# Row sums and pooled products of an attention kernel on 64x64 tiles of TensorE

## The chip, the cores and the metric

One core of a Trainium2 chip runs the whole program. The metric is the device time of one execution in microseconds; lower is better. The engines are TensorE (PE), VectorE (DVE), ScalarE (ACT), GpSimd (POOL) and SyncE (SP), which run side by side and wait for one another through semaphores. PEld is TensorE's loading of weights.

## The reference

The kernel computes two kinds of attention, adds them, and sends the sum through a feed-forward block. There are 8 batches with 8 heads, 576 positions and a head dimension of 64.

```python
def _attn_ref(q, k, v):                       # (8, 8, 576, 64)
    factor, scale = 4, 1 / sqrt(64)
    q_d, k_d, v_d = (x.reshape(B, H, 144, 4, D).mean(axis=3) for x in (q, k, v))
    out_up = np.repeat(sm_attn(q_d, k_d, v_d), 4, axis=2)   # attention of the pooled positions
    mask = np.abs(pos[:, None] - pos[None, :]) < factor     # a band of 7 positions
    scores = np.where(mask, scale * q @ k.T, -1e9)
    out_local = softmax(scores) @ v
    return out_up + out_local

def _moe_ref(x, w_in, w_out):                 # x: (4608, 512), d_ff 2048
    h = x @ w_in
    return (h * sigmoid(h)) @ w_out
```

## The kernel before

**Pairs.** Two heads are worked on together and called a pair; there are 32, p = 0 to 31, four to a batch. All matmuls of the attention are small and use parts of TensorE's array: a matmul on a 64x64 tile takes 64 rows of keys (or of the head dimension) and 64 output columns. In the code `half(j)` is the lower or upper 64 partitions.

For each pair TensorE transposes q and k (`pe_T`, into the PSUM banks `o0` and `pe_`), multiplies them (`pe_S`, into the banks A and B, which are the tile `AB`), and later multiplies the exponentials with v (`pe_main`). ScalarE copies the transposed k out (`ek`) and takes the exponentials `Pt` of the banded scores (unit `x`) and `Pd` of the pooled scores (unit `xd`). VectorE copies the transposed q out of `o0` (unit `eq`, line 362, `qT<-o`), pools k and q (`mk`, `mq`, lines 586 and 590) and multiplies `Pt` by the band's mask (unit `k`, line 628).

**The part that the change touches.** `pe_main` writes the banks C and D (the tile `CD`, 2 x 512 floats in each partition), which are the only ones for this from pair 4 on. For pair `pv` it multiplies the exponentials with v: 4 matmuls of the pooled remainder and 20 of the band, all on 64x64 tiles, where each half j of the keys has its own bank j; and then 4 "pooled products" that take all 128 keys at once (128x64 tiles, `vd[n][:, 2 * h, :]`). For pair `z` it forms the row sums of the exponentials with 14 matmuls against constant matrices of ones (`ohf`, `ohl`, `ohp`, `ohe`), also on 128x64 tiles, into columns 360 to 432 of bank C.

From the row sums, `after_Z` takes the reciprocal on VectorE (unit `r`, line 717 from pair 10 on, the constant `NDIR`), and ScalarE's queue writes it to a scratch tensor in DRAM (unit `z`, `scr<-zr`) and reads it back spread over the partitions (unit `b`, twice, `Rb<-scr`); the read is issued by ScalarE's queue after the write has landed, so what stands behind it on ScalarE waits too. For pairs below 10 another path without DRAM is used. `after_PV` multiplies the contents of C and D by `Rb` on VectorE into `xo` (unit `m`, line 745, 2 x 360 columns in one operation), and GpSimd adds the local and the pooled part into `xT` (unit `a`, line 769).

**The feed-forward block.** `g1(j, f)` multiplies 512 tokens of `xT` by 128 columns of `w_in` (4 matmuls into one of two banks `HP`), ScalarE takes the tanh (unit `t`, line 783), and VectorE forms the gated value (unit `s`, line 785, `gT<-th,HP`), which frees the bank. `g2` multiplies by `w_out`, four parts of 4 matmuls, into `o0` (or `pe_` for some of the last tokens); ScalarE copies the result out (unit `o`, line 800) and SyncE stores it.

**The order of the work.** From n = 10 on a step V(n) puts S(n), T(n+1), PV(n-2) and Z(n-1) into one unit on TensorE, in this order of matmuls: scores of pair n, transposes of pair n+1, products of pair n-2, row sums of pair n-1, pooled products of pair n-2. Between two steps stand about four `g1` units and the four parts of one `g2`; in steps up to V14 also a unit VP or RB. Every unit has a guessed cost, and a planner (`Plan.order`) plays through the program with these costs and gives each engine its list of units; the engines then run their lists in order. A list of names in `FIRST` fixes the beginning of an engine's list. Before the change `FIRST` is empty.

In the profile, all matmuls but the transposes stand at line 359, the transposes at line 572, and all DMA issues at line 464.

Of the kernel before, what the change touches and what calls it, by code (L numbers as in the profile page):

```python
# [6 lines left out]
ALU = mybir.AluOpType  # L7
# [12 lines left out]
NDIR = 10  # L20
# [141 lines left out]


FIRST = {
}

class Plan:
# [109 lines left out]
def bass_hourglass_attn__then__act_silu_kernel(  # L277
# [9 lines left out]
    with kctx:  # L287
        E = kctx.enter_context
        L = Plan()
        res = {}  # L290

        def R(name, psum=False):
            if name not in res:
                res[name] = Res(name, psum)
            return res[name]
# [5 lines left out]
        NQK, NVS, NVQ, NB, NX, NT, NP_, NV, NR = 4, 4, 2, 3, 2, 2, 4, 4, 3  # L301
# [13 lines left out]
        vd = sb("vd", [128, 4, 64], BF16, NV)  # L315
# [4 lines left out]
        Pt = sb("Pt", [128, 2, 288], BF16, NP_)  # L320
        Pd = sb("Pd", [128, 2, 216], BF16, NP_)
        zr = sb("zr", [128, 72], F32, 2)
        Rb = sb("Rb", [128, 720], F32, NR)
        xo = sb("xo", [128, 2, 360], F32, NX)
# [10 lines left out]
        ohl = sb("ohl", [128, 127], BF16)  # L335
        ohf = sb("ohf", [128, 64], BF16)
        ohp = sb("ohp", [128, 127], BF16)
        ohe = sb("ohe", [128, 64], BF16)
# [14 lines left out]
        def one(eng, name, cost, fn, r=(), w=(), dma=None, prio=None, dcost=0.0):  # L353
            u = L.unit(eng, name, cost, prio, dcost)
            L.op(u, fn, r, w, dma)
            return u

        def mm(u, out_, lhsT, rhs, r, w, start=True, stop=True):
            L.op(u, lambda t: t.matmul(out_, lhsT, rhs, start=start, stop=stop, skip_group_check=True), r, w)  # L359
# [6 lines left out]
        def half(j):  # L366
            return slice(64 * j, 64 * j + 64)
# [282 lines left out]
        def acc(p):  # L650
            return (HP, rH) if p < 4 and p % 2 else (CD_, rCD_)

        def pe_main(u, pv, z):
            fresh = set()

            def first(x, h):
                f = (x, h) not in fresh
                fresh.add((x, h))
                return f

            if pv is not None:
                m, n = pv % NP_, pv % NV
                CD, rCD = acc(pv)
                rd = [R(f"vd{n}0"), R(f"vd{n}1"), R(f"Pd{m}")]
                for h in range(2):
                    for j in range(2):
                        mm(u, CD[half(h), j, 288:360], vd[n][half(j), 2 * h + 1, :], Pd[m][half(j), h, 144:216],
                           rd, [rCD[j]], start=first(j, h), stop=False)
                for i in range(5):
                    for h in range(2):  # L670
                        for j in range(2):
                            a, e = 58 * i, min(58 * i + 58, 288)
                            mm(u, CD[half(h), j, a:e], vb[n][half(j), 5 * h + i, :],
                               Pt[m][half(j), h, a:e], [R(f"vb{n}"), R(f"P{m}")], [rCD[j]],
                               start=False, stop=True)
            if z is not None:
                m = z % NP_
                CD, rCD = acc(z)
                for s in range(4):
                    for h in range(2):  # L680
                        mm(u, CD[half(h), 0, 360:432], ohl[:, 63 - s:127 - s] if s else ohf[:, :],
                           Pt[m][:, h, 72 * s:72 * s + 72],
                           [R("ohl0"), R("ohl1"), R("ohf0"), R("ohf1"), R(f"P{m}")], [rCD[0]],
                           start=first(0, h), stop=False)
                for y in range(2):
                    for h in range(2):
                        mm(u, CD[half(h), 0, 360:432], ohp[:, 59 - 5 * y:123 - 5 * y], Pd[m][:, h, 72 * y:72 * y + 72],
                           [R("ohp"), R(f"Pd{m}")], [rCD[0]], start=False, stop=False)
                for h in range(2):
                    mm(u, CD[half(h), 0, 360:432], ohe[:, :], Pd[m][:, h, 144:216],  # L690
                       [R("ohe0"), R("ohe1"), R(f"Pd{m}")], [rCD[0]], start=False, stop=True)
            if pv is not None:
                m, n = pv % NP_, pv % NV
                CD, rCD = acc(pv)
                for y in range(2):
                    for h in range(2):
                        mm(u, CD[half(h), y, 288:360], vd[n][:, 2 * h, :], Pd[m][:, h, 72 * y:72 * y + 72],
                           [R(f"vd{n}0"), R(f"vd{n}1"), R(f"Pd{m}")], [rCD[y]], start=False, stop=True)

        def after_Z(p):  # L700
            i, u = p % 2, p % NR
            CD, rCD = acc(p)
            if p < NDIR:
                (h, m, l), rp = [rpart[p % 2][:, k, :] for k in range(3)], rpr[p % 2]
                zs, rest, rz = zr[i][:, :], rrest[p % 2][:, :], R(f"rrest{p % 2}")
                sg = [R("sgn0"), R("sgn1")]
                one("DVE", f"r{p}", 0.56, lambda e: e.reciprocal(zs, CD[:, 0, 360:432]), r=rCD[:1], w=[R(f"zr{i}")],
                    prio=-400000)
                one("ACT", f"rh{p}", 0.25, lambda e: e.activation(h, zs, AF.Copy), r=[R(f"zr{i}")], w=[rp[0]],
                    prio=-400000)  # L710
                one("DVE", f"rx{p}", 0.2, lambda e: e.scalar_tensor_tensor(  # L711
                    rest, h, sgn[:, 0:1], zs, ALU.mult, ALU.add), r=[R(f"zr{i}"), rp[0]] + sg, w=[rz], prio=-400000)
                one("DVE", f"rm{p}", 0.15, lambda e: e.tensor_copy(m, rest), r=[rz], w=[rp[1]], prio=-400000)
                one("DVE", f"rl{p}", 0.2, lambda e: e.scalar_tensor_tensor(  # L714
                    l, m, sgn[:, 1:2], rest, ALU.mult, ALU.add), r=[rz, rp[1]] + sg, w=[rp[2]], prio=-400000)
                return
            one("DVE", f"r{p}", 0.56, lambda e: e.reciprocal(zr[i][:, :], CD[:, 0, 360:432]),
                r=rCD[:1], w=[R(f"zr{i}")], prio=-400000)
            eng = "ACT"
            dma(eng, f"z{p}", scr[u][0:74, :], zr[i][0:74, :], [R(f"scr{u}")], f"scr{u}", 0.2, r=[R(f"zr{i}")], prio=-500000)  # L720
            for h in range(2):
                src = bass.AP(tensor=scr[u].tensor, offset=scr[u].offset + 64 * h * 72, ap=[[0, 64], [1, 720]])
                dma(eng, f"b{p}", Rb[u][half(h), :], src, [R(f"Rb{u}{h}")], f"Rb{u}{h}", 0.85,
                    r=[R(f"scr{u}")], prio=-500000)
# [17 lines left out]
        def after_PV(p):  # L742
            u, x = p % NR, p % NX
            CD, rCD = acc(p)
            one("DVE", f"m{p}", 0.92, prio=-450000 if L.boost else None, r=rCD + [R(f"Rb{u}0"), R(f"Rb{u}1")], w=[R(f"xo{x}")], fn=lambda e: e.tensor_tensor(  # L745
                xo[x][:, :, :], CD[:, :, 0:360], Rb[u][:, :].rearrange("p (x n) -> p x n", x=2), ALU.mult))
            b, kc = divmod(p, 4)
            t = b * S_
            segs = []
            wrap = (t // XR + 1) * XR - t  # L750
            if wrap >= S_:
                segs.append((0, S_))
            else:
                cuts = sorted({0, 288, wrap, S_})
                segs += list(zip(cuts, cuts[1:]))
            for a, e_ in segs:
                n = e_ - a
                d0 = (t + a) % XR
                dst = xT[:, kc, d0:d0 + n].bitcast(F32R)
                if n == S_:  # L760
                    dst = dst.rearrange("p (y g r) -> p y g r", y=2, r=4)
                    in0 = xo[x][:, :, 0:288].rearrange("p y (g r) -> p y g r", r=4)
                    in1 = xo[x][:, :, 288:360].unsqueeze(3).to_broadcast([128, 2, 72, 4])
                else:
                    y, c = divmod(a, 288)
                    dst = dst.rearrange("p (g r) -> p g r", r=4)
                    in0 = xo[x][:, y, c:c + n].rearrange("p (g r) -> p g r", r=4)
                    in1 = xo[x][:, y, 288 + c // 4:288 + (c + n) // 4].unsqueeze(2).to_broadcast([128, n // 4, 4])
                one("POOL", f"a{p}", 0.15 + n * 0.0019, lambda g, dst=dst, in0=in0, in1=in1: g.tensor_tensor(  # L769
                    dst, in0, in1, ALU.add), r=[R(f"xo{x}")], w=xblk(kc, t + a, t + e_), prio=-200000)  # L770
# [147 lines left out]
        n = 10  # L918
# [54 lines left out]
```

The softmax here doesn't subtract the row's maximum and nothing guards it: scores larger than these inputs give would overflow.

## Time and profile before

| what | value |
|---|---|
| median of 4 runs | 356.66 us (355.72 to 357.14) |
| the profiled execution's own time | 356.28 us |
| its span, from first to last instruction | 354.5 us |
| mean granted clock of TensorE | 0.97 |
| busy: PE, DVE, ACT, POOL | 329.7, 227.3, 181.0, 156.6 us |
| VectorE's reciprocal, line 717 | 22 times, 606 ns each |
| VectorE's product, line 745 | 30 times on CD, 901 ns each |
| step from V19 to V20 (152.75 to 161.41 us) | 8.66 us |

The profile is of one execution. Busy time counts from the start to the end of an instruction; matmuls overlap one another, so a busy TensorE is not one at its peak. The windows give the busy time of each engine in a stretch. A row of the timeline merges neighbouring instructions of one kind: start, time, engine, line, operation, output<-input, tile rows*columns, shape, count, and in brackets the idle time before it and who ended it. "Step" below is the time from one V's first matmul to the next one's.

### The profile page before, as it was taken

To read this page: it belongs to the slowest core of one execution; us is meant where nothing else is said; L and a number is where in the kernel's file an instruction comes from. 1 tells how busy PE (TensorE), PEld (TensorE's weight loads), DVE (VectorE), ACT (ScalarE), POOL (GpSimd) and SP (SyncE) were. 2 spreads that over 40 slices of the span, in tenths; PEclk is the share of its full clock that TensorE was granted. 3 is DMA by queue.
4 is the path that set the end of the run, shared out by engine and by line. 5 is a ranking of instruction groups with operands and counts; after the bars stand their busy time and mean duration, and the time that the engine had idled before them with its cause. 6 is when DMAs were issued, how large, how long until landed. Compare 5 with 4: busy or idle time off the path is not lost.

```text
span 354.5 us, 11025 instructions
## 1 busy us (share of the span) xinstructions
PE 329.7 (93%) x4742; PEld 214.6 (61%) x4742; DVE 227.3 (64%) x392; ACT 181.0 (51%) x326; POOL 156.6 (44%) x203
## 2 busy tenths in 40 slices
PE   1575699999999999999999999999999999999996
PEld 0464577766666666666666666666655666666642
DVE  7587889876677787877777667777754433333400
ACT  2766478766554555554555454555534343434321
POOL 7876974362556575575467654755111100000000
PEclk9995589999999999999999999999999999999999
DMA  8889999956788777777887778773122000100012
GB/s 238 238 241 270 314 296 223 228 131 199 208 220 218 227 220 223 219 213 214 228 231 206 217 219 224 214 199 96 66 97 75 31 30 30 60 31 30 31 59 89
DMA packets 73506, 60.28 MB, mean 170 GB/s; under 512 B 47986, under 2 KB 55794, under 8 KB 73458
## 3 DMA queue, kind: packets, MB, share of 16 engines
q1 hardware_dynamic: 63818, 44.27, 46.5%
q10 hardware_dynamic: 5416, 9.02, 8.5%
q0 software_dynamic: 4224, 6.29, 7.7%
q8 instruction: 37, 0.61, 0.7%
q14 instruction: 11, 0.09, 0.1%
HBM read 51.76 MB, written 9.91 MB: 174 GB/s over the span
## 4 chain that ended last, share of the span: by engine, by line
PE 85%; DVE 7%; ACT 2%; POOL 2%; DMA 1%; issue 1%; ACTq 0%; DVEq 0%
PE HP L359 38%; PE o L359 27%; PE pe_ L359 8%; PE CD L359 5%; PE AB L359 4%; POOL xo L382 2%; PE o L572 1%; DMA scr<-zr 1%; DVE rrest L711 1%; DVE gT L785 1%; DVE rp L714 1%; DVE xo L745 1%; DVE Pt L628 1%; ACT th L783 1%; PE pe_ L572 1%
## 5 line engine op out<-in xcount | busy, mean ns | idle before, releaser
L359 PE MATMUL HP<-xT,w_in_sb 128*128 128x512 f32 x576 | 159.9, 416 | 1.0 <-DVE gT L785 0.9
L785 DVE SCALAR_TENSOR_TENSOR gT<-th,HP 128x512 bf16<-128x512 f32 x144 | 96.4, 684 | 99.3 <-ACT th L783 99.3
L359 PEld LDWEIGHTS HP<-xT,w_in_sb 128*128 128x128 f32 x576 | 106.0, 189 | 28.4 <-DVE gT L785 1.4
L783 ACT ACTIVATE th<-HP 128x512 f32<-128x512 f32 x144 | 85.9, 599 | 72.8 <-PE HP L359 71.0
L359 PE MATMUL o<-w_out_bf,gT 128*128 128x512 bf16 x464 | 107.0, 380 | 0.0
L359 PEld LDWEIGHTS o<-w_out_bf,gT 128*128 128x128 bf16 x464 | 42.6, 98 | 54.3 <-issue 7.8
L769 POOL TENSOR_TENSOR xT<-xo 128x576 fp32r<-128x576 f32 (+3 forms) x48 | 44.7, 945 | 43.7 <-DVE xo L745 43.6
L800 ACT ACTIVATE osb<-o 128x512 f32<-128x512 f32 x29 | 17.4, 599 | 63.4 <-PE o L359 52.3
L559 POOL TENSOR_TENSOR vt<-vq 128x512 f32<-128x512 f32 x18 | 23.0, 1280 | 55.0 <-DMA vq<-in_v_dram 55.0
L544 POOL CAST qkb<-qk 128x1152 bf16<-128x1152 f32 x30 | 34.6, 1154 | 8.1 <-PE pe_ L572 4.0
L745 DVE TENSOR_TENSOR xo<-CD,Rb 128x720 f32<-128x720 f32 x30 | 27.0, 901 | 1.2 <-ACT Rb L735 0.9
L359 PE MATMUL pe_<-w_out_bf,gT 128*128 128x512 bf16 x112 | 26.4, 380 | 0.0
L554 POOL CAST vb<-vs 128x640 bf16<-128x640 f32 x30 | 21.6, 720 | 10.3 <-PE CD L359 5.2
L572 PE MATMUL o<-idn,qkb 64*64 64x64 bf16 x576 | 17.8, 205 | 8.4 <-DVE qkb L539 6.3
L586 DVE TENSOR_REDUCE kd<-kT 128x144 bf16<-128x576 bf16 x32 | 23.4, 733 | 1.1 <-ACT kT L582 1.1
L582 ACT ACTIVATE kT<-pe_ 128x576 bf16<-128x576 bf16 x32 | 21.0, 657 | 1.6
L628 DVE TENSOR_TENSOR Pt<-Pt,mask_bf 128x576 bf16<-128x576 bf16 x32 | 21.3, 667 | 0.5 <-ACT Pt L624 0.5
L624 ACT ACTIVATE Pt<-AB 128x576 bf16<-128x576 f32 x32 | 20.8, 650 | 1.2 <-PE AB L359 1.2
L572 PEld LDWEIGHTS o<-idn,qkb 64*64 64x64 bf16 x576 | 14.3, 119 | 9.2 <-DVE qkb L539 6.3
L572 PE MATMUL pe_<-idn,qkb 64*64 64x64 bf16 x576 | 16.7, 205 | 1.9 <-DVE qkb L541 1.0
L359 PEld LDWEIGHTS pe_<-w_out_bf,gT 128*128 128x128 bf16 x112 | 10.0, 98 | 13.6 <-issue 3.2
L590 DVE TENSOR_REDUCE qd<-qT 128x144 bf16<-128x576 bf16 x24 | 17.8, 742 | 0.0
(79 smaller groups left out, 316.2 us busy)
## 6 DMA issues: line engine op xcount, KB each, us to landing
vs<-in_v_dram SPq DMA_DIRECT2D x126, 80.0 KB, 4.4
qk<-in_q_dram SPq DMA_DIRECT2D x32, 288.0 KB, 3.9
out_dram<-osb SPq DMA_DIRECT2D x36, 256.0 KB, 3.2
qk<-in_k_dram SPq DMA_DIRECT2D x30, 288.0 KB, 4.8
Rb<-scr ACTq DMA_DIRECT2D x44, 180.0 KB, 4.1
vq<-in_v_dram SPq DMA_DIRECT2D x18, 256.0 KB, 4.7
w_in_sb<-in_moe_w_in_dram POOLq DMA_DIRECT2D x4, 1024.0 KB, 10.0
w_out_bf<-in_moe_w_out_dram POOLq DMA_DIRECT2D x4, 512.0 KB, 10.5
```

Of the source, the lines that this page charges most:

```text
L359: L.op(u, lambda t: t.matmul(out_, lhsT, rhs, start=start, stop=stop, skip_group_check=True), r, w)
L544: one("POOL", f"c{p}", 1.15, lambda g: g.tensor_copy(qkb[j][:, :, :], qk[i][:, :, :]), r=[R(f"qk{i}0"), R(f"qk{i}1")], w=[R(f"qkb{j}0"), R ...
L554: one("POOL", f"cw{p}", 0.72, lambda g: g.tensor_copy(vb[m][:, :, :], vs[i][:, :, :]), r=rr, w=[R(f"vb{m}")])
L559: one("POOL", f"va{p}", 1.3, lambda g: g.tensor_tensor(vt[:, :, :], vq[i][:, :, 0:128], vq[i][:, :, 128:256], ALU.add), r=rr, w=[R("vt")])
L572: L.op(u, lambda e, o=o, w=w, j=j: e.transpose(o, w, idn[half(j), :]), [R("id"), R(f"qkb{n}{x}")], [rE if x else rF])
L582: one("ACT", f"ek{p}", 0.68, lambda e: e.activation(kT[j][:, 3:579].rearrange("p (g r) -> p g r", r=9), pe_[:, 0:288].bitcast(BF16).rearra ...
L586: one("DVE", f"mk{p}", 0.74, lambda e: e.tensor_reduce(kd[j][:, 0:SD], kT[j][:, 3:579].rearrange("p (g r) -> p g r", r=4), AX.X, ALU.add), ...
L628: one("DVE", f"k{p}", 0.46, lambda e: e.tensor_tensor(Pt[m][:, :, :], Pt[m][:, :, :], mask_bf[:, :].unsqueeze(1).to_broadcast([128, 2, 288 ...
L745: one("DVE", f"m{p}", 0.92, prio=-450000 if L.boost else None, r=rCD + [R(f"Rb{u}0"), R(f"Rb{u}1")], w=[R(f"xo{x}")], fn=lambda e: e.tenso ...
L769: one("POOL", f"a{p}", 0.15 + n * 0.0019, lambda g, dst=dst, in0=in0, in1=in1: g.tensor_tensor(dst, in0, in1, ALU.add), r=[R(f"xo{x}")], w ...
L783: one("ACT", f"t{j}_{f}", 0.62, lambda e: e.activation(th[tb][:, :], hps[hb], AF.Tanh, scale=0.5), r=[rH[hb]], w=[R(f"th{tb}")], prio=-1)
L785: one("DVE", f"s{j}_{f}", 0.71, lambda e: e.scalar_tensor_tensor(gT[j % 2][:, f, :], th[tb][:, :], 1.0, hps[hb], ALU.add, ALU.mult), r=[rH ...
```

## The change

From pair 10 on, the row sums and the pooled products are formed on 64x64 tiles: each of the 18 matmuls becomes two, one for each half of the keys, and each half writes its own bank. Row sums now lie in columns 432 to 504 of both banks, pooled products in columns 288 to 432 of both (four matmuls of the pooled remainder move there as well). The pooled products now come before the row sums. VectorE adds the two halves: the unit `r` becomes copy, add, reciprocal; the unit `m` becomes copy, add and product of the pooled part, and the product of the rest. `FIRST` is filled with a list of names for each engine, up to the middle of step V11. The planner's cost of `r` goes from 0.56 to 0.9, that of `m` from 0.92 to 1.4.

```diff
 FIRST = {
+    "PE": """T0 T1 S0 T2 S1 Z0 ... V11 g1_1_6 g1_1_7 VP10 g2_0_1_0 g2_0_1_1""",
+    "ACT": ..., "DVE": ..., "POOL": ..., "SP": ...
 }
...
                 for h in range(2):
                     for j in range(2):
-                        mm(u, CD[half(h), j, 288:360], vd[n][half(j), 2 * h + 1, :], Pd[m][half(j), h, 144:216],
+                        c = 288 + 72 * j if pv >= NDIR else 288
+                        mm(u, CD[half(h), j, c:c + 72], vd[n][half(j), 2 * h + 1, :], Pd[m][half(j), h, 144:216],
                            rd, [rCD[j]], start=first(j, h), stop=False)
...
-            if z is not None:
+            if pv is not None and pv >= NDIR:
+                for y in range(2):
+                    for h in range(2):
+                        for j in range(2):
+                            mm(u, CD[half(h), j, 288 + 72 * y:360 + 72 * y], vd[n][half(j), 2 * h, :],
+                               Pd[m][half(j), h, 72 * y:72 * y + 72], rd, [rCD[j]], start=False, stop=True)
+            if z is not None and z >= NDIR:
+                ...
+                parts = [(ohl[:, 63 - s:127 - s] if s else ohf[:, :], Pt[m][:, :, 72 * s:72 * s + 72]) for s in range(4)]
+                parts += [(ohp[:, 59 - 5 * y:123 - 5 * y], Pd[m][:, :, 72 * y:72 * y + 72]) for y in range(2)]
+                parts.append((ohe[:, :], Pd[m][:, :, 144:216]))
+                for i, (o, x) in enumerate(parts):
+                    for h in range(2):
+                        for j in range(2):
+                            mm(u, CD[half(h), j, 432:504], o[half(j), :], x[half(j), h, :], ro, [rCD[j]],
+                               start=first(j, h), stop=i == 6)
+            elif z is not None:
...
-            if pv is not None:
+            if pv is not None and pv < NDIR:
...
-            one("DVE", f"r{p}", 0.56, lambda e: e.reciprocal(zr[i][:, :], CD[:, 0, 360:432]),
-                r=rCD[:1], w=[R(f"zr{i}")], prio=-400000)
+            q = L.unit("DVE", f"r{p}", 0.9, -400000)
+            L.op(q, lambda e: e.tensor_copy(zr[i][:, :], CD[:, 0, 432:504]), rCD[:1], [R(f"zr{i}")])
+            L.op(q, lambda e: e.tensor_tensor(zr[i][:, :], zr[i][:, :], CD[:, 1, 432:504], ALU.add),
+                 [R(f"zr{i}"), rCD[1]], [R(f"zr{i}")])
+            L.op(q, lambda e: e.reciprocal(zr[i][:, :], zr[i][:, :]), [R(f"zr{i}")], [R(f"zr{i}")])
...
+            q = L.unit("DVE", f"m{p}", 0.92 if p < NDIR else 1.4, -450000 if L.boost else None)
...
+                pool = [CD[:, j, 288:432].rearrange("p (y n) -> p y n", y=2) for j in range(2)]
+                xp = xo[x][:, :, 288:360]
+                L.op(q, lambda e: e.tensor_copy(xp, pool[0]), rCD[:1], wx)
+                L.op(q, lambda e: e.tensor_tensor(xp, xp, pool[1], ALU.add), [rCD[1]] + wx, wx)
+                L.op(q, lambda e: e.tensor_tensor(xp, xp, rb[:, :, 288:360], ALU.mult), rr + wx, wx)
+                L.op(q, lambda e: e.tensor_tensor(xo[x][:, :, 0:288], CD[:, :, 0:288], rb[:, :, 0:288], ALU.mult),
+                     rCD + rr, wx)
```

## The prediction

> **What bounds the kernel now.** I read the page first: is there an engine that never rests, and where?
>
> ```profile
> span 354.5 us, 11025 instructions
> ...
> PE   1575699999999999999999999999999999999996
> ...
> PEclk9995589999999999999999999999999999999999
> ...
> PE 85%; DVE 7%; ACT 2%; POOL 2%; DMA 1%; issue 1%; ACTq 0%; DVEq 0%
> ```
>
> From slice 7 (53 us) TensorE is busy in every slice, at a full granted clock, and is 85% of the chain that ended last. From there each microsecond taken from TensorE's own work is a microsecond of the span, unless another engine then comes late. I count on the span of 354.5 us; that execution took 356.28 us, 1.8 outside the span, which I leave unchanged. The median of the runs, 356.66, is 0.4 higher.
>
> The change acts in the stage of the steps V12 to V33, one every 8.65 us. The windows of two neighbouring steps show how much slack the others have:
>
> ```profile
> 152.75:161.41 8.66, 8.66 (x140) 5.60 (x140) 6.23 (x10) 4.04 (x9) 5.17 (x5) 1.00 0.80 226
> 161.41:170.10 8.69, 8.69 (x140) 5.61 (x139) 6.39 (x11) 4.94 (x10) 5.12 (x5) 1.00 0.82 216
> ```
>
> PE (second number) fills the step; VectorE (fourth) works 6.2 to 6.4 us, so some 2.3 us are free. Inside a step, the timeline of PE at the end of V19:
>
> ```profile
> 153.31 0.21 PE L359 MATMUL CD<-Pd,vd 64*64 64x72 bf16 x4
> 153.34 0.34 PE L359 MATMUL CD<-Pt,vb 64*64 64x58 bf16 x20
> 153.61 0.22 PE L359 MATMUL CD<-Pt,ohf 128*64 128x72 bf16 x2
> ...
> 153.86 0.23 PE L359 MATMUL CD<-Pd,vd 128*64 128x72 bf16 x4
> 154.03 0.50 PE L359 MATMUL HP<-xT,w_in_sb 128*128 128x512 f32 x1
> ```
>
> The single records show three things. The 24 matmuls on 64x64 tiles start in rounds of four, 32 ns apart, also the round with 72 columns (153.311 to 153.343). The last starts at 153.492, and then nothing starts until 153.613, where the 128x64 tiles begin. These start in nine pairs, the last at 153.894. A start-to-start gap of 119 to 122 ns stands at this turn in nearly every step. The turn into the 128x128 matmuls behind costs 128 ns from 128x64 and 123 to 141 ns from 64x64 (the two such places), so that one stays.
>
> **TensorE, part by part.** The change puts pool and row-sum matmuls on 64x64 tiles: 18 become 36, and the turn falls away.
> - The turn: the next round would have started at about 153.502 instead of 153.613: -0.111 us.
> - Streaming: nine pairs took 0.281 us from first to last start (the first step 52 ns, the rest 33); nine rounds of four at 32 ns take 0.256: -0.025. Bounds: never under the 31 ns a round that the transposes of the same step reach; above, if only two ran at a time as now, 18 steps of 33 ns, +0.30. I take 32 ns, since the round with 72 columns is the same shape with the same tile order.
> - Sum: -0.13 us a step. V12 to V33 lose the turn, 22 steps: -2.9 us. In V11 the pool part of pair 9 still has its turn, so nothing there. The lists in FIRST name units up to V11 in the order of the trace of before; nothing to gain or lose.
>
> The Trainium skill speaks against such splitting: "TensorEngine Tiling (Array Packing)", section Instruction Overhead, gives each matmul about 60 cycles whatever its columns, and warns against tiling a dimension that is already small. By an estimate from that page, 18 more matmuls charged one after the other at 2.4 GHz would add 0.45 us a step, some 10 us in all; the 32 ns rounds above say that four share that time.
>
> **VectorE.** Its step is back to back around the turn:
>
> ```profile
> 152.88 1.30 DVE L785 SCALAR_TENSOR_TENSOR gT<-th,HP 128x512 bf16<-128x512 f32 x2 [1.52 <-ACT th L783]
> 154.11 0.61 DVE L717 RECIPROCAL zr<-CD 128x72 f32<-128x72 f32 x1
> 154.63 0.70 DVE L362 COPY qT<-o 128x576 bf16<-128x576 bf16 x1
> ...
> 157.75 0.90 DVE L745 TENSOR_TENSOR xo<-CD,Rb 128x720 f32<-128x720 f32 x1
> 158.56 0.54 DVE L628 TENSOR_TENSOR Pt<-Pt,mask_bf 128x576 bf16<-128x576 bf16 x1
> ```
>
> The unit r (reciprocal) gets a copy and an add ahead of it. No row has these sizes. The product L745 (720 elements) takes 901 ns and L785 (512) 684, both reading PSUM: 217 ns for 208 elements, 1.04 ns each, and some 150 ns fixed, so 0.226 us for 72 elements. The copy L362 (576 elements in 694 ns) has 95 fixed: 0.17. So 0.17 to 0.23 for the copy, 0.23 for the add. Each result is read by the next one, which waits. How that looks, early in the kernel:
>
> ```profile
> 17.32 0.29 DVE L711 SCALAR_TENSOR_TENSOR rrest<-rp,sgn,zr 128x72 f32<-128x72 bf16 x1
> 17.65 0.73 DVE L713 CAST rp<-rrest 128x72 bf16<-128x72 f32 x1
> 18.41 0.29 DVE L714 SCALAR_TENSOR_TENSOR rp<-rp,sgn,rrest 128x72 bf16<-128x72 bf16 x1
> ```
>
> A dependent one starts 35 ns after the end of the last; independent ones start 80 ns before it (154.63 against 154.11 + 0.61). So r grows by 0.17..0.23 + 0.035 + 0.23 + 0.035 = 0.47 to 0.53 us; I take 0.50. Below, a reciprocal that reads SBUF instead of PSUM might be up to 0.1 shorter; above, with GpSimd busy the same small SBUF operations ran to 0.73 (L713, alone 0.18), so up to 0.8.
>
> The skill's "VectorE: DVE Perf Modes", section The DRAIN you can't avoid, says that a semaphore between chained operations costs nothing extra. The rows above show about 115 ns for each such wait; by the page r would grow by 0.27 only.
>
> The unit m becomes four dependent operations: 144-element copy 0.25 to 0.30, add 0.30, product 0.30, 576-element product 0.75, with three gaps of 0.035; 1.67 us to the next start instead of 0.82: +0.85, and up to 1 more in a step where its SBUF product meets GpSimd (L711, the same kind, ran from 0.28 to 3.25). Cover: the 2.3 us free behind the mask product in each step. r and m together take 1.35 of it. Behind m stand the mask product (read by the next V, 2 us later), GpSimd's sum into xT (wanted after the next V at the latest, with which it can change places), and the release of CD (next written 2.5 us later). I cost m at nothing; were its cover gone by 1 us more, the next step would start late by that.
>
> **Where r counts.** Behind r on VectorE stands the copy of qT out of bank o, which the second GEMM wants next. From the start of V: r starts at 1.35 us (the product ahead of it ends then, held by ScalarE's tanh, so an earlier end of V does not help it), the copy ends at 2.57, seen by PE 0.05 later; the GEMM's first matmul starts at 3.22 to 3.25. Slack 0.615. After the change the GEMM would start 0.13 earlier: slack 0.485 against a growth of 0.47 to 0.53. So a stall of 0 to 0.05, mean 0.02, in the 16 steps without VP (V12 to V14 have it between) and before V31: +0.3 us.
>
> Second, r releases the row-sum write to scr, on whose landing ScalarE's queue waits, with tanh behind it. The write was issued 2.0 us into V and landed at 4.6 to 5.2 mostly, at 6.8 to 6.9 in three steps. The chain of waits shows one:
>
> ```profile
> 198.04 4.93 DMA scr<-zr
> ...
> 204.79 0.49 ACT th L783
> ...
> 205.31 0.70 DVE gT L785
> ```
>
> A landing past about 6.3 delays the next step's tanh, gT, and r; there r started 0.4 to 0.5 late, which the slack of 0.615 swallowed. Now the write goes out at 2.5. In the three steps where that was so already (161.4, 204.7, 222.1) it landed at 5.6 to 5.9, in time. But if one lands at 7.4, 0.5 past those of now, r starts some 1.0 late (0.45, that 0.5, and the shorter step), and as its growth has used the slack, all of it reaches the GEMM. I allow one such step, a little under 1.0: +0.9.
>
> Sum: -2.9 + 0.3 + 0.9 = -1.7 us. On 356.28 this gives 354.6, on the median 355.0; I say 354.8.
>
> **The rivals.** *All of it is cover*: r grows under 0.485 and no landing is late: -2.9, 353.4 us. For it: the regular steps repeat to 10 ns and the sums meet almost exactly. *The landing decides* (the slower side): the scr write, now issued behind the q and k loads that SP starts at 2.0 and 2.4, lands past 6.3 in more steps. Each costs about 1.0; from four on the change is slower. Five: -2.9 + 0.3 + 5.0 = +2.4, 358.7 us. For it: the three landings at 6.8 to 6.9; against: the three writes issued late that landed in time. *r is too long*: at a growth of 0.8 the GEMM waits 0.315 in 16 steps, +5.0 - 2.9: 358.4 us; it turns slower at 0.67. Against: GpSimd is mostly idle 1.8 to 2.3 us into V. *The tiles don't overlap*: two at a time, (0.30 - 0.11) x 22 = +4.2, 360.5 us; the rounds of four speak against it.
>
> **How the numbers follow.** Forecast 0.35, all cover 0.28, landing 0.17, r too long 0.12, no overlap 0.05, else 0.03. A measurement of this kernel can tell about 0.3% (1.1 us) from no change. All of the cover case and most of the forecast are faster by more: 0.58; the forecast with a second late step and the landing case with three (+0.4) are within: 0.17; the rest slower: 0.25. Range 353.3 to 358.7: from all cover to five late landings. The likeliest case by itself: 353.8 to 356.
>
> **What would show it.** In the timeline of PE no gap between 64x58 and the next CD matmuls, all CD rows 64*64, rounds of 32 ns, the HP matmul 0.13 earlier after V starts. On VectorE the start of L362 about 2.37 us into V. In the list of waits, PE o on the qT copy: small. In steps with stalls, a chain through scr<-zr. Wrong if CD matmuls take over 1.0 us from first to last, if the GEMM starts later than 3.25 into V in most steps, or if steps V12 to V30 are not near 8.55 us.

## The result and the profile after

The changed kernel takes 358.5 us (median), the kernel before 357.2 in the same comparisons: a ratio of 1.0036, 95% interval [1.0022, 1.0051]. It is slower by 1.3 us, where a gain of 1.9 us was forecast. The profiled execution of after took 358.23 us with a span of 356.5 us (before: 356.28 and 354.5). From V10 to V31, which is the same work in both, the trace shows 183.06 us against 182.16; another execution of each gave 184.10 and 181.83. From V31 to the end it is 98.52 against 98.80. The stretch up to V10 varies from 72.8 to 76.8 us between executions with the same order of work there, so it says nothing on the change.

The page of after: span, PE by slices, and the engines' shares of the chain that ended last.

```profile
span 356.5 us, 11952 instructions
...
PE   0585599999999999999999999999999999999996
...
PE 84%; DVE 7%; ACT 3%; DMA 2%; SPq 2%; issue 1%; ACTq 1%; DVEq 0%
```

TensorE fills every slice from the sixth on. The step V19 in the windows (us; busy time of PE, PEld, DVE, ACT, POOL; clock, DMA share, GB/s):

```profile
153.97:162.64 8.67, 8.67 (x157) 5.51 (x157) 7.59 (x15) 4.49 (x8) 4.68 (x6) 1.00 0.85 215
```

VectorE (fourth number) went from 6.2 to 7.6 us of a step, and in the next step from 6.4 to 7.9; the step did not get shorter. The end of V, in the timeline of PE:

```profile
154.56 0.34 PE L393 MATMUL CD<-Pt,vb 64*64 64x58 bf16 x20
154.72 0.26 PE L393 MATMUL CD<-Pd,vd 64*64 64x72 bf16 x8
...
155.19 2.11 PE L393 MATMUL HP<-xT,w_in_sb 128*128 128x512 f32 x8
157.21 0.39 PE L393 MATMUL o<-w_out_bf,gT 128*128 128x512 bf16 x1
```

The turn is gone: the last `vb` matmul starts at 154.708, the next one at 154.718. All tiles in bank CD are 64*64. GEMM1 (the matmuls into `HP`) starts 1.22 us into V (V starts at 153.97) instead of 1.27. But GEMM2 (`o<-w_out_bf,gT`) starts at 3.24, as before, where the same step (V starts at 152.75) has it at 3.25:

```profile
156.00 0.39 PE L359 MATMUL o<-w_out_bf,gT 128*128 128x512 bf16 x1
```

The timeline of VectorE in the step of after says why:

```profile
155.34 0.23 DVE L771 COPY zr<-CD 128x72 f32<-128x72 f32 x1
155.68 0.23 DVE L772 TENSOR_TENSOR zr<-zr,CD 128x72 f32<-128x72 f32 x1
155.94 0.60 DVE L774 RECIPROCAL zr<-zr 128x72 f32<-128x72 f32 x1
156.46 0.69 DVE L396 COPY qT<-o 128x576 bf16<-128x576 bf16 x1
...
160.35 0.89 DVE L811 TENSOR_TENSOR xo<-xo,Rb 128x144 f32<-128x144 f32 x1
```

The four lines at the top are `r` and the copy of qT; the last is the product of the pooled part in `m`, which took 0.89 us. The first row of `r` starts 1.37 us into V (before: 1.35), but the copy of qT now ends at 3.19 instead of 2.57, and GEMM2 starts 0.06 behind it. The saving is over before GEMM2, and the copy of qT has become what releases it. The waits say the same (us, times, longest):

```profile
PEld o L393 <- DVE qT L396: 5.4, 16, 0.3
```

Before, this line had 0.8 us and 3 times. These 5.4 us are waits of the weight load, most of which lie beside the matmuls ahead.

### The profile page after: what moved, and what is told of

It is laid out like the page before. It is cut to its first block, busy times and chain, and to the rows that moved or that the text cites. A ratio compares the mean times of both kernels' runs of the same rounds, so it can differ in the third digit from the quotient of the medians.

```text
span 356.5 us, 11952 instructions
## 1 busy us (share of the span) xinstructions
PE 330.7 (93%) x5138; PEld 213.8 (60%) x5138; DVE 254.5 (71%) x502; ACT 179.0 (50%) x326; POOL 156.7 (44%) x203
## 4 chain that ended last, share of the span: by engine, by line
PE 84%; DVE 7%; ACT 3%; DMA 2%; SPq 2%; issue 1%; ACTq 1%; DVEq 0%
PE HP L393 37%; PE o L393 28%; PE pe_ L393 8%; PE CD L393 5%; PE AB L393 4%; SPq L498 2%; PE o L606 1%; DMA vs<-in_v_dram 1%; DVE gT L852 1%; DVE rrest L764 1%; DVE xo L805 1%; DVE rp L767 1%; DVE Pt L662 1%; DMA scr<-zr 1%; ACT th L850 1%
## 5 line engine op out<-in xcount | busy, mean ns | idle before, releaser
L393 PE MATMUL HP<-xT,w_in_sb 128*128 128x512 f32 x576 | 165.6, 423 | 0.9 <-DVE gT L852 0.9
L850 ACT ACTIVATE th<-HP 128x512 f32<-128x512 f32 x144 | 84.0, 598 | 113.5 <-PE HP L393 94.8
L393 PE MATMUL o<-w_out_bf,gT 128*128 128x512 bf16 x464 | 109.6, 380 | 0.0
L393 PEld LDWEIGHTS o<-w_out_bf,gT 128*128 128x128 bf16 x464 | 41.3, 98 | 56.0 <-issue 8.4
L836 POOL TENSOR_TENSOR xT<-xo 128x576 fp32r<-128x576 f32 (+3 forms) x48 | 44.8, 947 | 56.0 <-DVE xo L812 39.3
L662 DVE TENSOR_TENSOR Pt<-Pt,mask_bf 128x576 bf16<-128x576 bf16 x32 | 18.4, 575 | 1.4 <-ACT Pt L658 1.4
L812 DVE TENSOR_TENSOR xo<-CD,Rb 128x576 f32<-128x576 f32 x22 | 16.7, 758 | 0.8
```

Of the source, the lines that this page charges most:

```text
L662: one("DVE", f"k{p}", 0.46, lambda e: e.tensor_tensor(Pt[m][:, :, :], Pt[m][:, :, :], mask_bf[:, :].unsqueeze(1).to_broadcast([128, 2, 288 ...
L850: one("ACT", f"t{j}_{f}", 0.62, lambda e: e.activation(th[tb][:, :], hps[hb], AF.Tanh, scale=0.5), r=[rH[hb]], w=[R(f"th{tb}")], prio=-1)
```

## The experiments

"New order" below is the order of units that the planner makes with the change's costs; "old order" is that of before. Where a kernel is to run in one of them, all five lists of `FIRST` hold it in full.

**The two kernels again.** One more profiled execution of before, and twelve more executions of the change. "Regular steps" below is the median length of the steps V15 to V30.

> The kernel before once more, for what repeats. If a step's times are set by the program, steps V15 to V30 come out at 8.62 to 8.66 us again and V10 to the end at 281.0 us within 0.3; the opening up to V10 (73.5 us in one profile, 74.9 in that of the change, with the same lists) may differ by 1 us or more from run to run, and then says nothing on the change.

> The change again, for the ratio on the same chip as e15 to e17: 1.002 to 1.005; steps V15 to V30 8.66 to 8.68 with the GEMM at 3.24 to 3.25 in nearly all of them, V14 losing about 0.9; perhaps a step with a late landing, since e6 and e5 had some.

Before: V10 to V31 181.83, regular steps 8.63 (8.65 in its first trace), V10 to the end 280.6, a little under what was expected. The change: ratio 1.0026 [1.0001, 1.0051], regular steps 8.67 again, but now with three long steps: V15 9.17, V23 8.81, V27 9.28, which the first trace of it had not. So the loss has a part that repeats and a part that changes from execution to execution.

**Order alone, work alone.** The order of after with the operations of before, and the reverse.

```diff
 # order alone: before, with
-FIRST = {}
+FIRST = {...}   # the new order in full
 # work alone: after, with
-FIRST = {...}   # up to V11; the planner goes on with r 0.9, m 1.4
+FIRST = {...}   # the old order in full
```

> The work of before in the order of the change (all five lists fixed to it). Theory 'gate' (the longer r on VectorE holds back the qT copy and so the second GEMM): no cost, V10 to the end 281.0 us as before, steps 8.62 to 8.66, since r is short again. Rival 'order' (the new lists are what costs): V10 to the end 281.5 to 282, with 0.5 us or more lost in V13 and V14. Rival 'landing': the scr write goes out at 2.0 us into V, so whatever V14 lost to its landing shrinks from 0.9 to about 0.3.

> The work of the change in the order of before. 'Gate': the GEMM still starts 3.24 us into V, steps 8.65 to 8.67, V10 to the end 280.9 to 281.3. 'Order': the 0.055 us that each V is shorter comes through, steps 8.60, V10 to the end 279.8. 'Landing': late steps as in before (three with r 0.4 late), each now with 0.4 to 1.0 us lost, V10 to the end above 282.

> The work of before in the order of the change, again. From its trace (V10 to V31 0.7 to 1.0 us longer than before) the ratio should be 1.000 to 1.003; from its first ratio, 0.996. A second 0.996 would mean that executions without a profile gain from the order what the trace does not show.

Order alone gave 0.9957 [0.9927, 0.9987] and, run a second time, 1.0008 [0.9975, 1.0041]. The traces show 182.88 and 182.84 from V10 to V31, 0.7 to 1.1 more than before, with regular steps of 8.66; V10 to the end is 281.7, as the rival 'order' expected. So the traces show a loss by the order; the two timings show none. They hardly meet, which shows how far one comparison of this kernel may be off, and what the order costs in time stays open.

Work alone, in the old order, is slower: 1.0081 [1.0050, 1.0112], V10 to V31 186.80. GEMM2 starts at 3.24 here too, as 'gate' expected. Its steps are 8.65, except V13 9.61, V17 10.14, V22 10.76 and V25 9.37 (V21 and V29 have one GEMM1 part fewer in the old order, and V22 one more, which makes it 9.55 before). The chain of waits through V17:

```profile
138.49 0.19 DVE zr L836
...
143.45 1.07 DVE xo L876
...
145.38 1.36 POOL xT L901
...
146.78 0.51 PE HP L458
```

`r` (L836) delays `m` (L874 to L877), one product of which takes 1.07 us; GpSimd's sum into xT waits for it, and a GEMM1 part that the old order has ahead of V waits for that sum: 1.5 us lost. In the new order no step of the change shows this wait: its own new costs in the planner spare it.

**TensorE's part alone**, in the old and in the new order. It leaves the adding of the halves out: `r` and `m` are single operations as before, on part of the sums.

```diff
-            L.op(q, ... tensor_copy ...); L.op(q, ... tensor_tensor ... ALU.add ...)
-            L.op(q, lambda e: e.reciprocal(zr[i][:, :], zr[i][:, :]), ...)
+            one("DVE", f"r{p}", 0.56, lambda e: e.reciprocal(zr[i][:, :], CD[:, 0, 432:504]), r=rCD, ...)
...
+            L.op(q, lambda e: e.tensor_tensor(xo[x][:, :, :], CD[:, :, 0:360], rb, ALU.mult), rCD + rr, wx)
```

> TensorE's half of the change alone, in the order of before: matmuls as in the change, but VectorE takes bank C's row sums and columns 288 to 360 of both banks as they are (the sums over the two halves are left out, and the constant ohf is all ones so that no row sum is zero). 'Gate': r is short again, the GEMM starts 3.17 to 3.20 into V, steps 8.57 to 8.60, V10 to the end 279.8 to 280.0, ratio 0.996 to 0.997. If TensorE's saving is not real (its exit into the next GEMM or the streaming gives it back): steps 8.62 to 8.66, ratio 1.000.

> TensorE's half alone in the order of the change (all lists fixed to it); VectorE as in before, so the sums over the two key halves are left out and ohf is all ones. Against the work of before in this order (182.9 us from V10 to V31, steps V15 to V30 8.64 to 8.68): theory 'gate' expects every V 0.055 us shorter and nothing given back, the GEMM 3.17 to 3.20 into V, steps 8.59 to 8.62, V10 to V31 181.7 to 181.9, ratio about 0.997 of that order's. A rival in which the order's alternation of the two GEMMs takes the saving expects steps of 8.65.

Old order: 0.9966 [0.9935, 0.9996], regular steps 8.58. GEMM2 starts 3.18 us into V, here in the step that starts at 153.44:

```profile
156.61 0.39 PE L458 MATMUL o<-w_out_bf,gT 128*128 128x512 bf16 x1
```

New order: 0.9970 [0.9938, 1.0002], steps 8.63 against 8.66 for the order alone, GEMM2 at 3.20. That is between what the two theories expected: part of the saving is lost in the new order. TensorE's part alone is thus worth about 0.06 us a step in the old order and 0.04 in the new one; the ratio in the old order is 1.2 us (0.0034 of 357.8), with an interval from 0.1 to 2.3. From V10 to V31 both traces show 181.99. In the new order that is 0.9 less than the order alone; in the old one it is no gain on before (182.16 and 181.83), since V13 takes 9.06 instead of 8.23 or 8.13, behind a load of v for GpSimd that took 5.03 us.

**VectorE's part alone**, in the new order: TensorE as before, `r` and `m` with as many operations as in the change (the added ones repeat a read of the same values).

```diff
+            L.op(q, lambda e: e.tensor_copy(zr[i][:, :], CD[:, 0, 360:432]), ...)
+            L.op(q, lambda e: e.tensor_tensor(zr[i][:, :], zr[i][:, :], CD[:, 0, 360:432], ALU.max), ...)
+            L.op(q, lambda e: e.reciprocal(zr[i][:, :], zr[i][:, :]), ...)
```

> VectorE's half alone in the order of the change: matmuls of before, r as copy, maximum with itself, reciprocal, m as copy, maximum with itself and two products, so that the values stay those of before and the lengths are those of the change. 'Gate': the qT copy ends 3.2 us into V and the GEMM, due at 3.22 to 3.25, is just not or hardly held, steps 8.66 to 8.70; V14 loses 0.9 to 1.0 (with 0.56 for the order alone); V10 to V31 183.1 to 183.6. If VectorE's extra work is what makes the change slow by itself: steps over 8.75 and V10 to V31 over 184.5.

1.0030 [1.0002, 1.0058], regular steps 8.65, V14 9.85, V18 9.00, V27 8.95; V10 to V31 183.46 against 182.9 for the order alone. The copy of qT ends 3.10 us into V, not 3.2, and GEMM2 is not held (3.23). For `r` grew by 0.52 here and by 0.60 in the change: its second operation reads bank C again and waits for the copy alone, and it starts 0.035 us after it, where the change's add, which also waits for bank D, starts 0.104 after (155.34 + 0.23 to 155.68 above). In the step that starts at 152.13:

```profile
153.48 0.23 DVE L817 COPY zr<-CD 128x72 f32<-128x72 f32 x1
153.75 0.23 DVE L818 TENSOR_TENSOR zr<-zr,CD 128x72 f32<-128x72 f32 x1
```

So with no saving on TensorE this growth fits into the slack of `r`, and what is lost stands in single late steps.

**Is it the copy of qT behind `r`?** Two ways to end it sooner: set it ahead of `r`, or make `r` shorter with one reduction over both banks.

```diff
 # qT first: in the list of VectorE
-  r12 eq14 ... r13 eq15 ...
+  eq14 r12 ... eq15 r13 ...
 # reduction (and the same for the pooled part of m)
-            L.op(q, ... tensor_copy(zr[i][:, :], CD[:, 0, 432:504]) ...)
-            L.op(q, ... tensor_tensor(zr[i][:, :], zr[i][:, :], CD[:, 1, 432:504], ALU.add) ...)
+            L.op(q, lambda e: e.tensor_reduce(zr[i][:, :], CD[:, :, 432:504].rearrange("p j n -> p n j"), AX.X, ALU.add), rCD, ...)
```

> The change, with the qT copy ahead of r on VectorE from V11 on. 'Gate': the GEMM is let go, 3.17 to 3.20 into V, steps 8.59 to 8.62; the scr write goes out 0.6 later, at 3.2, lands at 6.2 to 7.0, and V14 loses 0.6 more than the 0.9 of the change, so V10 to V31 182.3 to 182.8 (183.1 in the change). Rival 'landing' (the write's landing decides): steps with late landings in V15 to V30, over 9 us, V10 to V31 above 183.5.

> The change, with the copy and the add of r put into one reduction over the two banks, likewise in m. r should grow by 0.30 to 0.37 instead of 0.60: 144 elements read from PSUM, 0.30 us, and one wait. 'Gate': the qT copy ends at 2.9 and the GEMM starts 3.17 to 3.20 into V, steps 8.59 to 8.62, V14 loses 0.7 to 0.8, V10 to V31 181.9 to 182.2. If the reduction over two banks is slow (over 0.5 us), the GEMM stays held as in the change, steps 8.66.

The reduction, timeline of VectorE in one step (V starts at 163.55):

```profile
164.93 0.31 DVE L836 TENSOR_REDUCE zr<-CD 128x72 f32<-128x144 f32 x1
165.27 0.60 DVE L838 RECIPROCAL zr<-zr 128x72 f32<-128x72 f32 x1
165.79 0.70 DVE L461 COPY qT<-o 128x576 bf16<-128x576 bf16 x1
```

The copy of qT ends 2.94 us into V instead of 3.19, GEMM2 starts at 3.17, and the regular steps are 8.60 instead of 8.67, with TensorE's matmuls unchanged. That shows the gate. The time was 0.9988 [0.9958, 1.0019], about that of before. Its trace (an execution of 359.97 us; the median is 357.93) has three late steps (V19 9.59, V23 9.48, V27 9.30), so V10 to V31 took 184.47, where 181.9 to 182.2 were expected.

With qT first GEMM2 also comes early (3.20, regular steps 8.63), but the time is 1.0117 [1.0067, 1.0167]: `r` now ends at 3.2, its write goes out later, and in the execution traced V16 to V20 take 9.2 to 9.4 us each; V10 to V31 is 188.1, far over what 'gate' alone expected, as the rival 'landing' had it. The chain of waits through one of them:

```profile
133.91 0.61 DVE zr L839
...
134.55 3.94 DMA scr<-zr
...
138.51 0.47 ACTq L563
```

The write to scr, its landing, the two reads issued by ScalarE's queue (ACTq, the second for 0.62 us), then its tanh or copy-out, gT, and the next `r`: a closed ring in which each step is as long as the ring. Here the landing decides.

**Taking the landing off ScalarE's queue.** The reads of scr issued by SyncE instead, with the reduction, with before, with the change, and with the order alone; and both halves read by one DMA.

```diff
-                dma(eng, f"b{p}", Rb[u][half(h), :], src, ...)
+                dma("SP", f"b{p}", Rb[u][half(h), :], src, ...)
 # one read:
+            src = bass.AP(tensor=scr[u].tensor, offset=scr[u].offset, ap=[[64 * 72, 2], [0, 64], [1, 720]])
+            dma(eng, f"b{p}", Rb[u][:, :], src, ...)
```

> The change with the reduction over both banks, and with the two reads of scr issued by SyncE instead of ScalarE, so that nobody on ScalarE waits for the write's landing; ScalarE's, TensorE's, VectorE's and GpSimd's orders as in the change. Theory 'gate and landing' (each holds back part of TensorE's saving): steps V15 to V30 all 8.59 to 8.61, none over 8.8, V14 loses only the 0.56 that the order itself costs, V10 to V31 181.6 to 181.9 us, ratio 0.995 to 0.998. If SyncE's loads, now behind these reads, are late: GpSimd's casts wait longer and steps over 8.8 appear again.

> Before, with the two reads of scr issued by SyncE, all other orders as before. In before the landings of up to 6.9 us were swallowed by the slack of r; so 'gate and landing' expects next to nothing: steps 8.62 to 8.66, V10 to V31 181.8 to 182.1, ratio 0.997 to 1.000. If landings cost before too in executions that no profile showed, the ratio is under 0.997.

> The change itself, with the two reads of scr issued by SyncE. 'Gate and landing': the landing's part goes (V14 loses 0.5 to 0.6 instead of 0.9, no step over 8.8 in V15 to V30), the gate's part stays (the GEMM 3.24 into V, steps 8.66 to 8.67); V10 to V31 182.6 to 182.8, ratio 1.000 to 1.002. If only the landing made the change slow: ratio under 0.998.

> The work of before in the order of the change, with the two reads of scr issued by SyncE. 'Gate and landing': steps 8.64 to 8.68 without exception, V14 loses 0.5, V10 to V31 182.5 to 182.8, ratio 0.998 to 1.002. If the new order by itself is better than the old one, as the ratio of 0.996 without this edit might say against its trace: 0.996 or less again.

> The change with the reduction over both banks (r short), the two reads of scr put into one DMA, and that read issued behind the next tanh on ScalarE (in V13 behind the copy-out of the GEMM), so that a landing up to 7.2 us into V holds nobody up. 'Gate and landing': steps V15 to V30 8.59 to 8.62, at most one over 8.8 (three with 0.7 to 1.0 us lost in e6), V14 loses 0.5 to 0.6; V10 to V31 181.6 to 182.0 us against 184.5 in e6; ratio 0.995 to 0.998. If steps over 9 us remain, something else than ScalarE's wait made them.

> The change with its long r, and with the one read of scr issued later as in e15. 'Gate and landing': the GEMM stays at 3.24 us into V and the steps at 8.66 to 8.67, V14 loses 0.6 instead of 0.9, V10 to V31 182.6 to 182.9, ratio 1.000 to 1.002. If the landing was all of the loss: ratio 0.997.

All six missed. On SyncE: 1.0350 [1.0303, 1.0397], 1.0399 [1.0350, 1.0448], 1.0365 [1.0330, 1.0400] and 1.0280 [1.0235, 1.0324]. In the list that I wrote for SyncE the reads of pair 28 stand ahead of the loads of v for pair 31 and of the reads of pair 27. In the first of these runs SyncE stood from 235.2 to 246.4 us, until the row sums of pair 28 had landed, and only then issued the rest, at about 0.6 us each; the last load of v landed at 256.7, and GpSimd and GEMM1 waited for it. Step V30 alone takes 17 to 20 us in the four runs, 8 to 11 more than a regular one, and so most of the loss. It is a fault of that list. Some other steps lost time too, so these runs settle nothing on the landing. The regular steps kept their lengths (8.60 with the reduction, 8.67 the change).

One read for both halves: 1.3005 [1.2955, 1.3055] and 1.2984, steps of 13.7 us. The chain of waits is the same ring, and the landing of the write is nearly all of it:

```profile
149.38 10.45 DMA scr<-zr
```

In the trace of the packets, the 2880-byte packets of one read run at most three or four at a time and need 9 to 12 us in this kernel; with two reads of 64 rows each (the changed kernel), up to 11 to 18 run at a time and they need 1.9 to 4.2 us. The write above lands late because it stands behind a read on the same queue: that read's packets run from 147.3 to 158.3, and the write's own start at 158.2. So these two runs settle nothing on the landing either.

**A better order.** In the new order the GEMM2 parts alternate with GEMM1 parts at the end of a step, and ScalarE has the copy-out behind the reads. The last two kernels set the four GEMM2 parts together again from V14 to V30 and the copy-out ahead of the reads, once with the reduction and once with the change's `r`.

```diff
-  V15 g1_2_4 g1_2_5 g2_1_1_0 g2_1_1_1 g2_1_1_2 g1_2_6 g2_1_1_3 g1_2_7 V16     # PE
+  V15 g1_2_4 g1_2_5 g2_1_1_0 g2_1_1_1 g2_1_1_2 g2_1_1_3 g1_2_6 g1_2_7 V16
-  xd15 b14 b14.1 t2_6 o1_1 t2_7                                               # ACT
+  xd15 o1_1 b14 b14.1 t2_6 t2_7
```

> The new order, with V14 to V30 regrouped as before (two GEMM1 parts, the four GEMM2 parts together, two GEMM1 parts, V), and on ScalarE the GEMM2 copy-out set ahead of the two scr reads; the unit r has one reduction over both banks in place of copy and add. If r's length and the landing in front of the copy-out explain the loss: qT copy ends 2.9 to 3.0 us into V, GEMM2 at 3.17, regular steps 8.57 to 8.60, V14 loses 0.5 to 0.6, at most one step over 8.8, V10 to V31 181.4 to 181.9 us (before: 181.8 to 182.2), ratio 0.995 to 0.999. Rival (the late steps do not come from the copy-out behind the landing): steps over 9.2 remain, V10 to V31 183 or more, ratio 0.999 or more.

> The same lists as in the regrouped order, with the change's own r (copy, add, reciprocal). If the gate and the landing explain the loss: GEMM2 at 3.24, steps 8.64 to 8.66, V14 loses 0.5 to 0.6, no step over 9.0, V10 to V31 182.3 to 182.8 us, ratio 1.000 to 1.002, so slower than the regrouped kernel with the reduction by about 1 us. Rival (order and landing cost nothing beyond the gate, or the late steps have another cause): V10 to V31 183.0 to 184.1 and a ratio of 1.0026 or more, as the changed kernel has.

With the reduction 0.9958 [0.9929, 0.9988]; with the change's `r` 1.0039 [1.0002, 1.0075]. They ran on the same chip beside the same runs of before, and differ only in the reduction, in `r` and in `m`: it is worth 2.4 us by the medians (356.49 and 358.88), 0.7%. Regular steps are 8.59 and 8.65, GEMM2 at 3.18 and 3.24, as expected. V10 to V31 is 182.80 and 184.17, 1.4 us apart and both above what I had expected: the first has V14 at 10.45 and V23 at 8.92, the second V15 at 9.40, V18 at 8.89 and V27 at 9.48. The chain from the second's V26 into V27 (starts at 222.19):

```profile
221.02 1.50 ACTq L563
...
222.57 0.61 ACT th L915
...
223.20 1.28 DVE gT L917 x2
224.48 0.15 DVE zr L836
```

One read took 1.50 us to issue where most take 0.45 to 0.62, and tanh, gT and `r` stood behind it. So late steps are not only a matter of the copy-out's place: here tanh, which stands behind the reads, came late instead. The kernel with the reduction is the fastest of those that compute everything; its interval excludes no change, but order alone had the same ratio once and did not repeat it, and its trace shows the gain in the regular steps (0.06 us each) and not in the whole of V10 to V31. That it beats the kernel before is likely, not settled.

## Why the prediction was wrong

Three terms of the sum failed. TensorE's saving was forecast at 2.9 us and is 1.2. The stall of GEMM2 was forecast at 0.3 us in all and takes back the whole saving in the regular steps. The lists were put at nothing, and the traces show a loss there. Of the signs that I had named, the regular steps (8.67 us, not near 8.55) say the same.

**The turn: right.** It went as forecast, and the tiles share TensorE in rounds of four; the rival that they don't overlap is out. By the page on "TensorEngine Tiling (Array Packing)" of the Trainium skill, section Instruction Overhead, which gives each matmul about 60 cycles of overhead, an estimate is a step grown by 0.45 us; GEMM1 started 0.055 earlier, so the trace speaks against charging those cycles one after the other.

**Streaming: mis-sized.** I took 0.256 us from the first start of the first round of four to that of the ninth. It is 0.300: rounds of 72 columns come every 34 ns or so, not 32, with one step of 50 ns (behind `ohf`; the pairs of before had 52 there, which I read and left out) and two of 42. The last round's four starts lie over 0.025 us, and the turn into GEMM1 costs 0.144 instead of 0.128, so GEMM1 comes 0.169 behind the last round's first start where it was 0.132 behind the last pair's. From the first CD matmul to GEMM1 it is 0.660 us against 0.715: -0.055 a step where -0.13 was forecast, 1.2 us in 22 steps and not 2.9. TensorE's part alone in the old order had the same size, in its steps and in its ratio.

**`r`: mis-sized, and decisive.** I took 0.50 us of growth; it is 0.60, and as `r` also starts 0.015 later, the copy of qT ends 0.61 later. Copy (0.23, the upper end of what I had given it) and add (0.23) were right. The gap ahead of the add was not: 0.10 us instead of 0.035. The add waits for two things, the copy and bank D, and a separate wait instruction of VectorE's sequencer (DVEq, 0.02 us in the chain, with 0.03 and 0.04 around it) stands between. VectorE's part alone, whose second operation waits for one thing, had the 0.035. With the saving at its true size, the slack was 0.615 - 0.055 = 0.56, and the copy's delay of 0.61 exceeds it by 0.05; against TensorE's part alone GEMM2 starts 0.07 later (3.245 and 3.176, medians). So each regular step stalls by what it had saved. The rival "`r` is too long" was the right mechanism with the wrong price: I had it decide at a growth of 0.67 against a saving of 0.13. By the Trainium skill's "VectorE: DVE Perf Modes", section The DRAIN you can't avoid, a semaphore in a chain costs nothing extra; by an estimate from that, `r` would have grown by 0.27 and all would have been cover. The measured 0.60 differs, and decides.

**"Nothing to gain or lose" in the lists: wrong.** I read `FIRST` only up to V11. Behind V11 the planner goes on with the new costs of `r` and `m`, and its order changes: a GEMM1 part moves behind V, V13 keeps two of them, and V14's transposes must wait for the copy-out of GEMM2. In the order-alone trace V14 ends its matmuls 1.90 us in instead of 1.34; in that of after 2.20, because a read's issue stands in front of the copy-out (the chain of waits of after):

```profile
104.88 2.90 DMA scr<-zr
...
107.80 0.45 ACTq L498
...
108.28 1.52 ACTq L498
...
109.91 0.61 ACT osb L867
```

That step is 0.6 to 0.9 us longer, 0.4 to 0.7 together with V12 and V13 at equal work (the new order has one GEMM1 part, 0.93 us, fewer there). The alternation of GEMM1 and GEMM2 adds 0.02 us in each of 16 steps, 0.3 to 0.4; regrouped, with the change's `r`, the regular steps are 8.65 and not 8.67. All of this is from traces: the two timings of the order alone, 1.5 us faster and 0.3 slower than before, do not show it.

**`m` at nothing: wrong for the order I assumed, right for the one that ran.** `m` grew by 0.97 where its SBUF product was undisturbed, not 0.85, since that product starts 0.13 after the add, and by 1.55 in the step shown, where it met GpSimd. In the old order three steps (V13, V17, V22; 8.23, 8.66 and 9.55 before) took 1.2 to 1.5 us more each; in V13 `m` is not all of it, since that step was 0.8 longer with TensorE's part alone too. "Can change places with V" happened only because the planner was told: that `m` cost nothing in the regular steps of the change was luck.

**The landing: right as a mechanism, partly as a size.** The write went out at 2.61 us. In the profiled execution of after no step past V14 is long; the second execution lost about 1.2 us in three (0.50 + 0.14 + 0.61). My one late step at 0.9 lies between the two by luck: only V15 came behind a late landing, V23 and V27 behind a read that took 1.5 us to issue. I did not see that such an issue does the same as a late landing.

Sum as the traces show it: regular steps 0 from the saving and +0.4 from the order, V12 to V14 +0.4 to 0.7, late steps 0 to 1.2, the end (V31 on) -0.3: +0.5 to +2.0 us, against 1.3 and 0.9 measured. That the saving does not come through is shown; how the loss of about 1 us is shared between the order and the late steps is not settled. The 0.35 for the forecast and 0.28 for all cover leaned on a margin (0.485 against 0.50) smaller than the error of either term.

## What to carry to other kernels

When a saving on the bounding engine has to pass a gate that another engine opens, compare the gate's slack with the growth on that engine, and give both a margin: here a stall of some 0.06 us a step took back the whole saving. Count dependent operations by their waits too, above all an operation that waits for two sources; one reduction over both banks costs 0.31 us where copy, wait and add took 0.57. And where an edit changes the costs in a planner, predict the order it will make before costing the edit in the old one.

## What the runs showed of the hardware

An operation of VectorE that waits for two things (the operation before it and a PSUM bank) got a wait instruction of its own and started 0.104 us after the end of the one before, in all 22 pairs of after; with one wait, in VectorE's part alone, it was 0.035 in all 22. The product of `m`, which waits for the add and for the reads of scr, started 0.13 after the add.

VectorE's product of two SBUF operands ran from 0.31 to 1.31 us for one shape (min, median, max in ns):

```profile
L811 DVE TENSOR_TENSOR xo<-xo,Rb x22: 307/403/1306, 99.7 to 277.9; 128x144 f32<-128x144 f32 x22
```

The other rows of `m`, which read PSUM, kept within 7 ns. The Trainium skill's "SBUF — State Buffer", section SBUF: two separate sides, has VectorE and GpSimd exclude each other on a shared port pair for operations with two SBUF inputs; the trace agrees. The seven products that met no GpSimd operation took 0.31 us. Each of the twelve that took longer than 0.32 began while GpSimd was in an operation, and ended 0.16 to 0.17 us after that operation did.

A DMA whose outermost dimension is 2 moved 360 KB in 9 to 12 us with at most three or four packets at a time, where two DMAs of 64 rows each had up to 11 to 18. The Trainium skill's "DMA: Bandwidth & Descriptors", section Why a DMA increments its semaphore by 16 and not by 1, says that the number of engines follows from the outermost dimension's size; the trace agrees.

By the chains of waits, the landing of the same 20.8 KB write varied from 1.9 to 5.4 us after its issue. The issue of the same read on ScalarE's queue took from 0.45 to 2.25 us (the longest in the kernel with the reduction). In after, the first read went out from 1.9 to 3.9 us after the write in the steps V15 to V29, whose lengths agree within 0.02 us.
